# A two-layer linear-attention and expert-selection network on one Trainium2 core: x of tiles 0 and 1 loaded ahead of the weights, their products taken together by weight blocks, state products of two tiles side by side, and the emission order of all stages written anew

## The chip, the cores and the metric

The kernel runs on one NeuronCore of a Trainium2 chip. The metric is the device time of one launch in microseconds (us). Before the change it is 745.13 us, the median of three runs (744.25 to 745.64). TensorE (PE) multiplies, VectorE (DVE), ScalarE (ACT) and GpSimd (POOL) do the elementwise work, SyncE (SP) issues the DMAs. PEld is PE's weight load, which overlaps its matmuls.

## The reference

Four sublayers act on x of 2048 rows and 576 columns: A, B, A, B, with the same weights in both rounds.

```python
def _A_ref(x, wqkv, wo):            # 32 heads of 18
    q, k, v = split_heads(x @ wqkv)
    pq, pk = phi(q), phi(k)         # phi(t) = where(t > 0, t + 1, exp(t)) + 1e-6
    kv = einsum("bhsd,bhse->bhde", pk, v)
    z = einsum("bhsd->bhd", pk)
    num = einsum("bhqd,bhde->bhqe", pq, kv)
    den = einsum("bhqd,bhd->bhq", pq, z)[..., None] + 1e-6
    return merge_heads(num / den) @ wo

def _B_ref(x, w_q, k1, k2, u, v):   # 32 heads, 8 x 8 experts, the best one of each
    s1 = (x @ w_q)[..., :dk] @ k1.T ; s2 = (x @ w_q)[..., dk:] @ k2.T
    e = argmax(s1) * 8 + argmax(s2)
    act = gelu(einsum("nd,nhkd->nhk", x, u[e]))
    return einsum("nhk,nhkd->nd", act, v[e])

x = x + _A_ref(_layernorm(x), A_wqkv, A_wo)
x = x + _B_ref(_layernorm(x), B_w_q, B_k1, B_k2, B_u, B_v)
x = x + _A_ref(_layernorm(x), A_wqkv, A_wo)
x = x + _B_ref(_layernorm(x), B_w_q, B_k1, B_k2, B_u, B_v)
```

The state kv is a sum over all 2048 rows, so the second half of a sublayer A can begin only when the first half is done with every tile.

## The kernel before

The 2048 rows are 16 tiles of 128 rows. Every operand of a product is split into a high part and a low part (`split`, lines 108 to 111: ACT writes the high part, DVE or POOL subtracts it for the low one), and a product is high by high, low by high and high by low: 14 passes of two matmuls each (`product`, lines 213 to 222). The 576 contracted columns are five blocks; block 2 holds 64 columns, its high part in the upper half of the partitions and its low part in the lower half, so that it needs one pass fewer. A weight block reaches its place by a DMA into a staging tile `wst` and a split into `whi` and `wlo`.

For a tile t of layer l the first half ("front") has these pieces. `front_T` (`fT`) transposes the normalised tile on PE (tile `ptf`, line 205) and splits the result into `thif` and `tlof`. `front_k`, `front_v` and `front_q` (`k`, `v`, `q`) form the products `ppk`, `ppv` and `ppq` (line 220); after k and q comes `phi` (lines 226 to 228: Exp on ACT, two DVE instructions) with the results `ek` and `eq`, and v is copied by ACT into one of the two buffers `v5` by the parity of t (lines 251 and 253). `front_state` (`st`, line 291) adds the tile's state product into PSUM tile `kva`: 20 small matmuls whose stationary operand is 128 x 64, where the other products have 128 x 128.

The second half ("back") has `state_mask` (`mk`), `state_sum` (`zs`, tile `z`), `state_fold` (`M`, tile `m`: the state times wo), `back_scale` (`num`: POOL and DVE, result `o`), `back_oT` (`oT`: transposes `pto`) and `back_out` (`O`: product `ppo`, residual, layernorm). Sublayer B has `exp_T` (`bc`: transposes `ptb` of the normalised tile t and of the gate `cg` of tile c), `exp_scores` (`S`: tile `pps`, or the upper half of `kva`, line 444), `exp_gelu` (`gel`), `exp_select` (`sel`: fourteen DVE instructions, the last writes `cg`, line 509) and `exp_out` (`po`). Where a piece yields, its later parts (evictions, splits) are emitted at a later mention of it.

The expert projection is multiplied with k1 and k2 by the kernel itself (`fold_load`, `fold_mm`, `fold_out`, `fold_T`): 64 loads of 288 KB from `in_wq_t`, eight in each of the front's tiles 2 to 9, and small matmuls (line 560) with a stationary operand of 128 x 32.

The order on the engines is the order of emission: `in_order` (lines 150 to 161) chains the instructions of PE, ACT, DVE and POOL one after the other. SP issues its DMAs in the order that the program gives them, each when its staging tile is free, so that a DMA that waits holds those behind it. The order is written by hand in three forms: the start (lines 697 to 734), a loop over the front's tiles 2 to 12 (lines 736 to 761) and texts that `play` (line 676) reads, a word per piece. `step2` (lines 682 to 690), run for s from 5 to 12, does the back of layer 0 for tiles s to s+2 and the front of layer 1 for tile s-3.

PSUM holds four tiles of 1024 columns (`ps`), `kva` one of them while a front runs.

## Time and profile before

| what | us |
|---|---|
| median of the three runs | 745.13 |
| the profiled execution: its own time | 744.04 |
| its span, first to last instruction | 742.2 |
| PE busy in it | 723.5 |
| DVE, ACT, POOL busy | 458.6, 289.7, 200.3 |
| granted TensorE clock, mean | 0.999 |

Read it so: PE is busy for 97% of the span, and the remaining 18.7 us are spread over the start, the changes from one stage to the next, and the end. The stages, by time: the start with tiles 0 and 1 to about 36 us, the front of layer 0 to about 222, the turn to the back with the first tiles to about 306, the eight steps to about 446, the turn to layer 1's back to about 540, and that back to the end. The rows of the profile follow where they are used. A "timeline" row gives the start, the duration, engine, line, what is written from what, the shapes, how many instructions are merged, and in brackets the engine's idle time before and what ended it.

### The profile page before, as it was taken

How to read it: one execution, taken by the hardware profiler on the slowest of the kernel's cores; microseconds unless marked ns; L12 is line 12 of the kernel's file. 1: busy time of each engine (PE TensorE's matmuls, PEld its weight loads, DVE VectorE, ACT ScalarE, POOL GpSimd, SP SyncE). 2: the span in 40 equal slices, each digit the busy share in tenths (PEclk: the TensorE clock that was granted, in tenths of full speed). 3: DMA queues.
4: the chain of work that ended last, by engine and by line, in shares of the span. 5: the costliest groups of instructions: out<-in, count | busy, mean ns of one | idle time of the engine just before them, and what ended most of it. 6: DMA issues, size and time to landing. Idle time of an engine off the chain costs nothing.

```text
span 742.2 us, 14654 instructions
## 1 busy us (share of the span) xinstructions
PE 723.5 (97%) x5672; PEld 673.6 (91%) x5672; DVE 458.6 (62%) x1006; ACT 289.7 (39%) x588; POOL 200.3 (27%) x541
## 2 busy tenths in 40 slices
PE   7999999999999999999999999999999999999995
PEld 5999989999998898999999999999899999999884
DVE  4532342324337886666666665662466899999986
ACT  5422333223234545444444444352333433444343
POOL 2210000001003543333333333230033334433431
PEclk9999999999999999999999999999999999999999
DMA  9736456631121322223332222212624323121101
GB/s 267 259 114 240 160 181 235 212 114 49 49 64 35 110 100 79 90 85 89 107 107 85 84 85 92 71 61 69 180 85 120 105 84 116 37 90 34 49 33 65
DMA packets 52470, 79.64 MB, mean 107 GB/s; under 512 B 5616, under 2 KB 22512, under 8 KB 52400
## 3 DMA queue, kind: packets, MB, share of 16 engines
q1 hardware_dynamic: 52400, 78.70, 33.3%
q8 instruction: 45, 0.74, 0.4%
q14 instruction: 25, 0.20, 0.1%
HBM read 55.12 MB, written 23.56 MB: 106 GB/s over the span
## 4 chain that ended last, share of the span: by engine, by line
PE 82%; DVE 10%; ACT 3%; issue 2%; POOL 1%; DMA 1%; SPq 0%; DVEq 0%; POOLq 0%; ACTq 0%
PE ppk L220 15%; PE ppv L220 15%; PE ppq L220 13%; PE ppo L414 13%; PE pps L444 6%; PE kva L444 5%; PE kva L291 3%; PE fold_ps L560 2%; PE ptb L205 2%; PE ptf L205 2%; PE pto L205 2%; PE po L528 2%; PE m L345 1%; DVE o L392 1%; DVE tlob L111 1%
## 5 line engine op out<-in xcount | busy, mean ns | idle before, releaser
L227 DVE TENSOR_SCALAR ek<-ek 128x576 f32<-128x576 f32 x32 | 14.7, 459 | 82.4 <-ACT ek L226 82.4
L220 PE MATMUL ppk<-whi,thif 128*128 128x252 f32 x320 | 49.6, 299 | 2.1 <-ACT thif L110 2.0
L414 PE MATMUL ppo<-ohi,thio 126*128 126x252 f32 (+1 forms) x320 | 50.3, 299 | 0.1
L220 PEld LDWEIGHTS ppk<-whi,thif 128*128 128x128 f32 x320 | 44.0, 188 | 6.5 <-issue 3.3
L171 POOL TENSOR_SCALAR rsf<-mvf 128x1 f32<-128x1 f32 x16 | 3.0, 190 | 169.7 <-DVE mvf L169 169.5
L227 DVE TENSOR_SCALAR eq<-eq 128x576 f32<-128x576 f32 x32 | 15.6, 488 | 52.6 <-ACT eq L226 52.6
L220 PE MATMUL ppk<-whi,tlof 128*128 128x252 f32 x320 | 47.6, 293 | 0.3 <-DVE tlof L111 0.3
L220 PE MATMUL ppv<-whi,thif 128*128 128x252 f32 x320 | 47.4, 295 | 0.1
L220 PE MATMUL ppv<-whi,tlof 128*128 128x252 f32 x320 | 46.9, 293 | 0.0
L195 ACT ACTIVATE yb<-x,rsb 128x640 f32<-128x640 f32 x32 | 29.5, 923 | 44.1 <-POOL rsb L188 44.1
L414 PEld LDWEIGHTS ppo<-ohi,thio 126*128 126x128 f32 (+1 forms) x320 | 44.8, 189 | 1.1 <-DVE eq L228 0.3
L220 PEld LDWEIGHTS ppk<-whi,tlof 128*128 128x128 f32 x320 | 44.2, 188 | 0.5 <-DVE tlof L111 0.5
L220 PEld LDWEIGHTS ppv<-whi,thif 128*128 128x128 f32 x320 | 43.9, 188 | 0.4 <-ACT thif L110 0.3
L181 ACT ACTIVATE junk<-x,mb 128x576 bf16<-128x576 f32 x32 | 24.7, 770 | 49.5 <-POOL mb L180 46.2
L220 PEld LDWEIGHTS ppv<-whi,tlof 128*128 128x128 f32 x320 | 43.9, 188 | 0.0
L251 ACT ACTIVATE v<-ppv 128x252 f32<-128x252 f32 x64 | 20.9, 379 | 50.1 <-PE ppv L220 48.2
L220 PE MATMUL ppq<-whi 128*128 128x252 f32 (+1 forms) x260 | 39.6, 299 | 0.6 <-DVE eq L228 0.6
L414 PE MATMUL ppo<-olo,thio 126*128 126x252 f32 (+1 forms) x256 | 39.5, 293 | 0.0
L414 PE MATMUL ppo<-ohi,tloo 126*128 126x252 f32 (+1 forms) x256 | 39.4, 293 | 0.0
L220 PE MATMUL ppk<-wlo,thif 128*128 128x252 f32 (+1 forms) x256 | 39.1, 293 | 0.0
L226 ACT ACTIVATE eq<-ppq 128x576 f32<-128x576 f32 x32 | 20.7, 647 | 46.8 <-PE ppq L220 46.8
L404 DVE SCALAR_TENSOR_TENSOR x<-po,x 128x576 f32<-128x576 f32 x29 | 21.9, 754 | 27.4 <-PE po L528 26.4
(162 smaller groups left out, 1794.8 us busy)
## 6 DMA issues: line engine op xcount, KB each, us to landing
fold<-in_wq_t SPq DMA_DIRECT2D x64, 288.0 KB, 4.8
whi<-hl_d SPq DMA_DIRECT2D x26, 320.0 KB, 3.4
pq_d<-eq SPq DMA_DIRECT2D x19, 288.0 KB, 2.1
pq<-pq_d SPq DMA_DIRECT2D x19, 288.0 KB, 3.0
xf<-in_x SPq DMA_DIRECT2D x16, 288.0 KB, 5.4
x<-in_x SPq DMA_DIRECT2D x16, 288.0 KB, 2.9
x_d<-x SPq DMA_DIRECT2D x16, 288.0 KB, 2.4
x<-x_d SPq DMA_DIRECT2D x16, 288.0 KB, 2.8
```

What stands on the lines that cost most here:

```text
L181: nc.scalar.activation(junk, xt, AF.Square, bias=m[:, 0:1], accum_out=m[:, 1:2])
L195: nc.scalar.activation(y, x2, AF.Identity, scale=rs[:, 0:1], bias=rs[:, 1:2])
L205: nc.tensor.transpose(pt[:, b * P:(b + 1) * P], x, ident)
L220: nc.tensor.matmul(o[:, at:at + c1 - c0], tt[a == "lo"][:, b, :], wb[:, cols + c0:cols + c1], start=(i == 0), stop=(i == len(todo) - 1))
L226: nc.scalar.activation(e, row(p), AF.Exp)
L227: nc.vector.tensor_scalar(e, e, 1.0, EPS, op0=ALU.min, op1=ALU.add)
L251: nc.scalar.activation(vt[:, c:c + 4, :63], x.rearrange("p (c e) -> p c e", c=4), AF.Copy)
L291: nc.tensor.matmul(a[64 * h:64 * h + 64, c * 72:c * 72 + n], vt[:, 2 * c + h], fk[:, f0:f0 + n], start=(t == 0 and c == 0), stop=(t == NT ...
L404: nc.vector.scalar_tensor_tensor(y, row(p), 0.0, xt, op0=ALU.add, op1=ALU.add, accum_out=total)
L414: nc.tensor.matmul(p[:, at:at + c1 - c0], hl[a][:r, b], w[:r, c0:c1], start=(i == 0), stop=(i == len(todo) - 1))
L444: nc.tensor.matmul(p[:, :512], hl[a == "lo"][:, b, :], shi[:, b] if w == "hi" else slo[:, blocks(REM)[b][1]], start=(i == 0), stop=(i == l ...
L528: nc.tensor.matmul(p[:, at:at + c1 - c0], c[i], vmix[:, c0:c1], start=(i == 0 and not based), stop=(i == 1))
```

## The change

What it does:

- The start issues the load of x for tile 1 before the first weight block, not after the fifth. `statistics` computes the factor and the offset on POOL for tiles 0 and 1 too, and the normalisation of tile 1 is on DVE instead of ACT. Both tiles are transposed before the products begin.
- k, v and q of tiles 0 and 1 are formed by `pair_product`: the passes are sorted by weight block, and each pass is done for tile 0 and then for tile 1 before the next.
- `st` of tile 1 and, in the loop over the tiles 2 to 9, of each odd tile stands right behind `st` of the even one before it. In the steps it does so too: two old steps make one text of double length, with both `st` in its second half.
- The loop ends with tile 9; tiles 10 to 12 are in the text behind it. All texts are new; most words keep their neighbours. On DVE, in the back of layer 1, `o` of tile 10, `phi` of tiles 11 and 12 and several subtractions and residuals stand some places earlier or later; PE's sequence there differs in the places of a few products and transposes.

```diff
+    def pair_product(t0, t1, cols, n, parts=PARTS):
+
+        o = [psum(f"pp{n}0_{t}") for t in (0, 1)]
+        todo = sorted(passes(REM), key=lambda p: p[1])
+        for i, (a, b, w) in enumerate(todo):
+            wb = whi[:, b] if w == "hi" else wlo[:, blocks(REM)[b][1]]
+            for p, tt in zip(o, (t0, t1)):
+                for c0, c1, at in parts:
+                    nc.tensor.matmul(p[:, at:at + c1 - c0], tt[a == "lo"][:, b, :], wb[:, cols + c0:cols + c1],
+                                     start=(i == 0), stop=(i == len(todo) - 1))
+        return o
...
     def front_k(l, t):
-        k = product(tt["f", l, t], whi, wlo, D, f"k{l}_{t}", by_block=(l == 0 and t == 0))
+        k = pairs.pop(("k", l, t), None)
+        if k is None:
+            k = product(tt["f", l, t], whi, wlo, D, f"k{l}_{t}")
         yield
         tt["fk", l, t] = phi(k, f"k{l}_{t}")
 
+    def front_pair(f, cols, parts=PARTS):
+        pairs[f, 0, 0], pairs[f, 0, 1] = pair_product(tt["f", 0, 0], tt["f", 0, 1], cols, f, parts)
...
-        nc.scalar.activation(y, x2, AF.Identity, scale=rs[:, 0:1], bias=rs[:, 1:2])
+        if vector:
+            nc.vector.tensor_scalar(y, x2, rs[:, 0:1], rs[:, 1:2], op0=ALU.mult, op1=ALU.add)
+        else:
+            nc.scalar.activation(y, x2, AF.Identity, scale=rs[:, 0:1], bias=rs[:, 1:2])
...
+    def pair(t):
+        return ((st, t - 1), (st, t)) if t % 2 else ()
...
     nc.sync.dma_start(ident, c_ident)
+    first_load(0, 1)
     wk_in = load_weight(wqkv, D, REM, "w")
-    first_load(0, 1)
     wv_in = load_weight(wqkv, 2 * D, REM, "w")
...
+        ys["f", 0, 0] = normalized(x0, rs0, "f0_0")
+        ys["f", 0, 1] = normalized(x1, rs1, "f0_1", vector=True)
         split_weight(wk_in, D, whi, wlo, REM, (0,))
...
+        run(0, (fT, 0), (fT, 1, 1))
+        split_weight(wk_in, D, whi, wlo, REM, (1,))
+        run(0, (fT, 1))
+        warm_up(2)
+        split_weight(wk_in, D, whi, wlo, REM, (2,))
         split_weight(wk_in, D, whi, wlo, REM, (3,), nc.gpsimd)
...
+        front_pair("k", D)
         split_weight(wv_in, 2 * D, whi, wlo, REM, (0, 1))
...
+        split_weight(wv_in, 2 * D, whi, wlo, REM, (4,))
+        front_pair("v", 2 * D, PARTS_V)
+        ys["f", 0, 2] = normalized(x2, next(st2), "f0_2")
...
+        front_pair("q", 0)
+        run(0, *pair(1), (q, 0), (q, 1))
+        PER, FIRST = 8, 10
...
-                run(0, (q, t), (fT, t + 1), (st, t))
...
+            run(0, (v, t), (q, t), (fT, t + 1), *pair(t))
...
-        for s in range(5, 13):
-            step2(s)
+        for s in range(5, 13, 2):
+            play("""
+            num0.2 k1.-3x2 v1.-3 num0.2x2 v1.-3 bc0.0,-1 v1.-3 fT1.-2 bc0.0,-1 fT1.-2 keep1.-2 oT0.1x2 S0.0x2 gel0.0
+            po0.-1x3 sel0.0 gel0.0 ld0.3 sel0.0 po0.-1 O0.1x4 sel0.0x2 num0.3 k1.-2x2 v1.-2 oT0.2 num0.3x2 v1.-2
+            bc0.1,0x2 v1.-2 st1.-3 st1.-2 fT1.-1x2 keep1.-1 oT0.2 S0.1x2 gel0.1 po0.0x2 ld0.4 po0.0 sel0.1 gel0.1
+            sel0.1 po0.0 O0.2x4 sel0.1x2
+        """, s)
```

The first place is the head of SP's queue. The names are the tiles written: `xf` is x of a tile, `wst` a staging tile of a weight block (two DMAs for block 2). Before:

```order
L599 DMA xf_152<-in_x 128x576
L699 DMA ident<-in_c_ident 128x128
L134 DMA wst_0_156<-in_wqkv 128x576
L134 DMA wst_1_158<-in_wqkv 128x576
L136 DMA wst_2_160<-in_wqkv 64x576
L137 DMA wst_2_160<-in_wqkv 64x576
L134 DMA wst_3_163<-in_wqkv 128x576
L134 DMA wst_4_165<-in_wqkv 128x576
L599 DMA xf_167<-in_x 128x576
```

And with the change:

```order
L625 DMA xf_152<-in_x 128x576
L717 DMA ident<-in_c_ident 128x128
L625 DMA xf_156<-in_x 128x576
L135 DMA wst_0_158<-in_wqkv 128x576
L135 DMA wst_1_160<-in_wqkv 128x576
L137 DMA wst_2_162<-in_wqkv 64x576
L138 DMA wst_2_162<-in_wqkv 64x576
```

The second x takes the third place, and every k weight block moves one place back.

The second place is PE in the steps, between the v product and the scores of a step. `ptb`, `ptf` and `pto` are transposes, `kva` from `ek` and `v5` is the state product, `kva` from `shi` and `thib` the scores. Before, with the step s = 7:

```order
L205 MATMUL ptb0_7_4294<-ident_66,yb0_7_4203 128x128 x5
L205 MATMUL ptb0_7_4294<-ident_66,cg0_6_4215 128x128
L205 MATMUL ptf1_5_4306<-ident_66,yf0_5_4162 128x128 x5
L291 MATMUL kva1_3582<-ek1_4_4252,v5_0_86 64x72 x8
L291 MATMUL kva1_3582<-ek1_4_4252,v5_0_86 64x36 x2
L205 MATMUL pto0_8_4328<-ident_66,o0_8_3990 128x128 x5
L444 MATMUL kva1_3582<-shi_80,thib0_7_4301 128x512 x5
```

With the change, s = 7, the first half of a double step:

```order
L209 MATMUL ptb0_7_4297<-ident_66,yb0_7_4210 128x128 x5
L209 MATMUL ptb0_7_4297<-ident_66,cg0_6_4222 128x128
L209 MATMUL ptf1_5_4307<-ident_66,yf0_5_4169 128x128 x5
L209 MATMUL pto0_8_4321<-ident_66,o0_8_3983 128x128 x5
L470 MATMUL kva1_3593<-shi_80,thib0_7_4304 128x512 x5
```

And s = 8, its second half:

```order
L209 MATMUL pto0_9_4509<-ident_66,o0_9_4224 128x128 x5
L209 MATMUL ptb0_8_4526<-ident_66,yb0_8_4431 128x128 x5
L209 MATMUL ptb0_8_4526<-ident_66,cg0_7_4443 128x128
L317 MATMUL kva1_3593<-ek1_4_4255,v5_0_86 64x72 x8
L317 MATMUL kva1_3593<-ek1_4_4255,v5_0_86 64x36 x2
L317 MATMUL kva1_3593<-ek1_5_4476,v5_1_87 64x72 x8
L317 MATMUL kva1_3593<-ek1_5_4476,v5_1_87 64x36 x2
L209 MATMUL ptf1_6_4558<-ident_66,yf0_6_4390 128x128 x5
L470 MATMUL kva1_3593<-shi_80,thib0_8_4533 128x512 x5
```

The state product of tile 4 has moved from the first half to the second, where it stands ahead of that of tile 5.

The third place is PE at the turn of layer 1, where the state is complete and is folded with wo (`m`) and summed (`z`). Before:

```order
L291 MATMUL kva1_3582<-ek1_15_6511,v5_1_87 64x72 x8
L291 MATMUL kva1_3582<-ek1_15_6511,v5_1_87 64x36 x2
L345 MATMUL m1_1_6577<-wob1_6468,kvb_83 126x288 x2
L327 MATMUL z1_6580<-zc_69,pick_68 128x4x72
L328 MATMUL z1_6580<-zc_69,pick_68 128x36
L327 MATMUL z1_6580<-zc_69,pick_68 128x4x54
L328 MATMUL z1_6580<-zc_69,pick_68 128x36
L345 MATMUL m1_4_6594<-wob4_6477,kvb_83 128x288 x2
```

With the change:

```order
L317 MATMUL kva1_3593<-ek1_14_6430,v5_0_86 64x72 x8
L317 MATMUL kva1_3593<-ek1_14_6430,v5_0_86 64x36 x2
L317 MATMUL kva1_3593<-ek1_15_6514,v5_1_87 64x72 x8
L317 MATMUL kva1_3593<-ek1_15_6514,v5_1_87 64x36 x2
L353 MATMUL z1_6584<-zc_69,pick_68 128x4x72
L354 MATMUL z1_6584<-zc_69,pick_68 128x36
L353 MATMUL z1_6584<-zc_69,pick_68 128x4x54
L354 MATMUL z1_6584<-zc_69,pick_68 128x36
L371 MATMUL m1_1_6592<-wob1_6389,kvb_83 126x288 x2
```

The four `z` matmuls now stand ahead of the first `m`, and the state product of tile 14 stands directly ahead of that of tile 15; before, the q product of tile 0 was between them.

More of the change, by code (lines that the diff above doesn't have):

```diff
@@ L211, in transposed, with product @@
         return hi, lo
-    def product(tt, hi, lo, cols, n, parts=PARTS, rem=REM, by_block=False):
+    def product(tt, hi, lo, cols, n, parts=PARTS, rem=REM):
         o = psum(f"pp{n}")
-        todo = sorted(passes(rem), key=lambda p: p[1]) if by_block else passes(rem)
+        todo = passes(rem)
         for i, (a, b, w) in enumerate(todo):
@@ L255, in front_q @@
     def front_q(l, t):
-        q = product(tt["f", l, t], whi, wlo, 0, f"q{l}_{t}")
+        q = pairs.pop(("q", l, t), None)
+        if q is None:
+            q = product(tt["f", l, t], whi, wlo, 0, f"q{l}_{t}")
         yield
@@ L734, in network @@
-        run(0, (st, 0), (fT, 2), (v, 1), (q, 0), (st, 1), (q, 1))
-        PER, FIRST = 8, 13
+        first_load(0, 3)
+        for t in v5:
+            nc.gpsimd.memset(t, 1.0)
+        split_weight(wv_in, 2 * D, whi, wlo, REM, (2,))
+        run(0, (k, 0))
+        split_weight(wv_in, 2 * D, whi, wlo, REM, (3,))
+        run(0, (k, 1))
+        x2 = xs.pop(("f", 2))
+        st2 = statistics(x2, "f0_2")
+        next(st2)
+        split_weight(wv_in, 2 * D, whi, wlo, REM, (4,))
+        front_pair("v", 2 * D, PARTS_V)
```

187 lines of the change are left out of this document (84 added, 103 removed).

## The prediction

> **What bounds the kernel now.** I read the page's head first, then a table of windows cut at the stages, then the chain of waits and the timelines of single places. In the table a row gives a stretch, its length, and each engine's busy time with its instructions.
>
> ```profile
> span 742.2 us, 14654 instructions
> PE 723.5 (97%) x5672; PEld 673.6 (91%) x5672; DVE 458.6 (62%) x1006; ACT 289.7 (39%) x588; POOL 200.3 (27%) x541
> ```
>
> ```profile
> core 0: us, PE busy (x) PEld busy (x) DVE busy (x) ACT busy (x) POOL busy (x), PEclk, DMA share, GB/s
> 0.00:36.00 36.00, 32.27 (x235) 26.70 (x236) 19.55 (x35) 17.97 (x31) 8.34 (x22) 1.00 0.87 271
> 36.00:160.00 124.00, 124.00 (x1191) 114.11 (x1190) 40.68 (x86) 36.88 (x86) 9.03 (x27) 1.00 0.55 184
> 160.00:300.00 140.00, 136.34 (x1062) 128.23 (x1062) 82.47 (x172) 55.05 (x113) 36.63 (x92) 1.00 0.22 69
> 300.00:446.00 146.00, 146.00 (x1165) 138.78 (x1165) 96.52 (x220) 65.92 (x134) 50.74 (x142) 1.00 0.28 92
> 446.00:540.00 94.00, 92.33 (x743) 87.69 (x742) 48.85 (x107) 37.89 (x78) 19.93 (x55) 1.00 0.33 97
> 540.00:690.00 150.00, 148.98 (x1029) 140.64 (x1028) 127.22 (x279) 55.76 (x108) 58.80 (x154) 1.00 0.27 83
> 690.00:742.00 52.00, 43.60 (x258) 37.44 (x256) 43.29 (x113) 20.27 (x40) 16.80 (x51) 0.99 0.13 46
> ```
>
> PE bounds every stage but the last. Its idle time is 3.7 us in the start, none in the fold loop and in the steps, 3.7 and 1.7 in the two turns, 1.0 and 8.4 behind 540. Since the change keeps the matmuls, it can gain in two ways: fewer such gaps, and less time lost when PE changes between kinds of matmul (which counts as busy). Behind 540 DVE is busy for 127 of 150 us and hands its lateness to the end; but from 446 to 540 it is busy for 49 of 94, so it is not behind when that stage begins, and what PE gains ahead of 540 moves DVE's work forward too.
>
> **The start.** Rows of PE, ACT, DVE and POOL, each from its timeline:
>
> ```profile
> 9.81 0.53 PE L220 MATMUL ppk<-whi,thif 128*128 128x252 f32 x2 [1.22 <-ACT thif L110]
> ...
> 14.35 0.71 PE L205 MATMUL ptf<-ident,yf 128*128 128x128 f32 x5
> 15.85 1.58 PE L220 MATMUL ppk<-whi,thif 128*128 128x252 f32 x10 [0.79 <-ACT thif L110]
> ```
>
> And from the chain of waits, the k product of tile 2 with its start and length:
>
> ```profile
> 36.74 3.64 PE ppk L220 x28
> ```
>
> ```profile
> 5.84 0.68 ACT L110 ACTIVATE whi<-wst 128x576 fp32r<-128x576 f32 x1 [3.83 <-DMA wst<-in_wqkv]
> ...
> 8.48 0.68 ACT L115 ACTIVATE whi<-wst 128x576 fp32r<-128x576 f32 x1 [0.52 <-DMA wst<-in_wqkv]
> ```
>
> ```profile
> 3.68 0.46 DVE L166 BATCH_NORM_STATS2 stf<-xf 128x6 f32<-128x288 f32 x1 [2.52 <-DMA xf<-in_x]
> ...
> 4.53 0.21 DVE L169 BATCH_NORM_AGGREGATE mvf<-stf 128x2 f32<-128x12 f32 x1
> ...
> 17.90 0.45 DVE L227 TENSOR_SCALAR ek<-ek 128x576 f32<-128x576 f32 x1
> ...
> 24.82 0.21 DVE L169 BATCH_NORM_AGGREGATE mvf<-stf 128x2 f32<-128x12 f32 x1
> ```
>
> ```profile
> 26.06 0.27 POOL L174 TENSOR_SCALAR rsf<-mvf,rsf 128x1 f32<-128x1 f32 x1
> ```
>
> Today tile 0's product starts at 9.81, halts with its weight blocks, and tile 1's transposes stand behind it with a second wait, 0.79. A product takes 3.64, a pass 3.64/14 = 0.26.
>
> With the change x of tile 1 is the third DMA, past the six of the k weight; today's third, a weight block, lets ACT start at 5.84. From then on: statistics 1.06 (3.68 to 4.53 + 0.21), POOL's three instructions 1.30 (25.03 to 26.33), the normalisation on DVE 0.5 (0.45 x 640/576, an estimate; twice that if it ran at half the rate), transposes and ACT's split 1.50 (14.35 to 15.85). Tile 1 can be multiplied at 5.84 + 1.06 + 1.30 + 0.5 + 1.5 = 10.2, say 10.3 with the waits between. The weight blocks come a place later. Blocks 0 and 2 land 2.64 apart today, 1.3 a block, so blocks 0, 1 and 2 now land near 7.2, 8.5 and 9.8, and the later ones at the same pace; a pair uses a block for six passes, 1.56, so none is late. Tile 1's low part waits in DVE's queue behind two weight splits: about 0.3. Then: pair k to 10.0 + 0.3 + 7.28 = 17.6, v to 24.9, transposes of tile 2 to 25.4, q to 32.7, the double state product 1.5 to 1.7: tile 2 starts at 34.4 to 34.7 on the scale on which it starts at 36.74. ACT's split of the first q block stands behind the normalisation of tile 2, which waits for statistics that DVE does behind `phi` of tile 1; by the same durations it ends at 25.0 to 25.3, just in time. I take **-2.0** and keep as ends -2.7 (neither the 0.3 nor a wait at q) and +0.6 (x of tile 1 lands no sooner than today's block 2, 8.48: 2.6 later).
>
> **State products side by side.** Rows of PE, of ACT and of the table of waits:
>
> ```profile
> 488.64 1.43 PE L291 MATMUL kva<-ek,v 128*64 128x72 f32 x40
> ```
>
> ```profile
> 349.94 0.86 PE L291 MATMUL kva<-ek,v 128*64 128x72 f32 x20
> 350.72 0.76 PE L205 MATMUL pto<-ident,o 128*128 128x128 f32 x5
> 351.24 1.40 PE L444 MATMUL kva<-shi,thib 128*128 128x512 f32 x5
> ```
>
> ```profile
> 349.50 0.81 ACT L110 ACTIVATE thib<-ptb 128x768 fp32r<-128x768 f32 x1
> 350.20 0.23 ACT L253 ACTIVATE v<-ppv 128x72 f32<-128x72 f32 x1
> 350.31 0.71 ACT L110 ACTIVATE thif<-ptf 128x640 fp32r<-128x640 f32 x1
> ```
>
> ```profile
> PEld kva L291 <- issue: 5.0, 30, 0.2
> ```
>
> The first row is a pair that the kernel already has, the next ones a single visit in a step, the last one PEld's waits. Twenty matmuls more cost 1.43 - 0.86 = 0.57, yet a visit occupies PE from 349.94 to 350.72, 0.78: some 0.12 to 0.2 is lost on leaving, and 5.0/30 = 0.17 on entering. A visit saved is worth 0.12 where the fold matmuls behind it (a third kind) pay the entry instead, else 0.29. Of 30 visits 19 remain: four go in the loop (**-0.5**), two in tiles 10 to 13 (**-0.6**), one at the turn of layer 1 (**-0.3**), four in the steps. In a first half without it the scores could start at 349.94 - 0.17 + 0.52 (from `pto` to the scores) = 350.29; ACT's split `thib` ends at 350.31 today, and the third copy of v (0.11 between the starts at 350.20 and 350.31) now stands ahead of it: 350.42 and a little, a wait of 0.17, with `thif` and `thio` queued behind it on ACT, which PE wants later. So a double step gains 0.12, the four **-0.5** (between 0 and -1.2).
>
> The Trainium skill, page TensorEngine Tiling (Array Packing), section Key Properties, says that a change of tiling mode, and not merely of the tile, drains the engine; its page TensorE: Matmul & The Clock Gate, section Single matmul latency, puts a drain near 175 ns. By these an estimate gives a visit 0.35 with both changes and 0.175 in the loop, and a sum 0.6 larger; the rows above show the entry at that price and the exit at less.
>
> **The turns.** Rows of PE's timeline, in the order in which they are used:
>
> ```profile
> 176.06 1.18 PE L220 MATMUL ppq<-whi,thif 128*128 128x252 f32 x7 [0.51 <-DVE ek L228]
> ```
>
> ```profile
> 259.95 0.30 PE L205 MATMUL ptb<-ident,cg 128*128 128x128 f32 x1 [0.87 <-DVE cg L509]
> ```
>
> ```profile
> 297.38 0.97 PE L444 MATMUL kva<-shi,thib 128*128 128x512 f32 x3 [0.70 <-ACT thib L110]
> ```
>
> ```profile
> 527.34 0.81 PE L291 MATMUL kva<-ek,v 128*64 128x72 f32 x20
> 529.70 1.21 PE L345 MATMUL m<-wob,kvb 127*126 127x288 f32 x4 [1.54 <-issue]
> ```
>
> ```profile
> 223.31 0.72 PE L327 MATMUL z<-zc,pick 128*128 128x288 f32 x2 [0.63 <-ACT zc L310]
> ...
> 224.60 3.16 PE L345 MATMUL m<-wob,kvb 127*126 127x288 f32 x12
> ```
>
> Tiles 10 to 12: the fold transposes move ahead of q, so that `ek` of tile 11 no longer shares ACT and DVE with their splits; the 0.51 should go: **-0.5** (0 to -0.65). At 259.95 PE waits for `cg`; now the 3.7 us product `ppo` of tile 3 stands ahead of it, and at 297.38 the transposes of tile 2 (0.5, today later) fill part of the 0.70. Together 1.4; but `po` of tile 0 then comes about 1.1 after the transposed `cg`, whose two splits wait behind others: **-1.0** (0 to -1.5). At 529.70 PE waits 1.54 for DVE's masked state with `z` still to do; in layer 0, where `z` goes first, it waits 0.63, does `z` in 1.29, and `m` follows without a wait: **-0.9** (0 to -1.2).
>
> **The sum.** -2.0 - 0.5 - 0.6 - 0.3 - 0.5 - 0.5 - 1.0 - 0.9 = -6.3. The new texts also reorder DVE, ACT and SP at some forty places, most with no effect; for one short new wait, of the size of those above, I give back 0.5: **-5.8**. The last stage I cost at nothing: DVE covers what PE gains there, and the same DVE work follows. If a moved DVE instruction waits, that cover is gone and the wait reaches the end whole. The profiled execution took 744.04, 1.1 below the median of 745.13; it becomes 738.2, and on the scale of the median **739.3**.
>
> **Rivals.** *The turns and the steps give nothing* (a filled wait returns at the next instruction: `thib` in the steps, `cg`'s split on DVE): the start, the loop and tiles 10 to 13 remain, -3.1, 742.0. For it: ACT's queue at 350.31 has no slack. Against: `z` ahead of `m` is shown by layer 0. Chance 0.15. *The start does not do what it says*, since x of tile 1 is as late as 8.48: -5.8 + 2.6, 742.0 to 742.5. For it: DMA is at 0.87 of its engines there. Against: the third load lands at 5.84. Chance 0.10. *All low ends together*: -2.7 - 0.5 - 0.6 - 0.3 - 1.2 - 0.65 - 1.5 - 1.2 = -8.6, 736.5. For it: no row forbids one of them. Against: eight at once. Chance 0.08. *Slower*: DVE's strict order in the last stage. There `o` of tile 10, `phi` of tiles 11 and 12 and several subtractions change places, and one that comes too early holds the whole queue; the longest DVE wait there now is this:
>
> ```profile
> DVE x L404 <- PE ppo L414: 4.7, 3, 3.3
> ```
>
> It decides from 7.3 us on (the 5.8 gained and the 1.5 of a measurable loss): three waits of 3.3, 745.13 - 5.8 + 9.9 = 749.2. For it: DVE has 23 us of slack in 150, so lateness isn't made up. Against: PE's order there is nearly the old one. Chance 0.09. A gain that stays within measurement, 0.04.
>
> **The numbers.** The forecast has 0.54. A change of 0.2%, 1.5 us, is what a measurement tells from none. Faster: 0.54 + 0.13 + 0.10 + 0.08 = 0.85; within: 0.02 of the first rival, 0.01 of the last, and 0.04: 0.07; slower 0.08. The range runs from a little below the best case, 736.2, to 743.6, the last measurable gain; the forecast's own is 737.5 to 741.
>
> **What would show it.** Right: a first pair at 10.0 to 10.4 and tile 2's k at 34 to 35; 40-matmul state products; the loop and steps still without a gap, a double step 0.1 to 0.3 shorter than two steps; `m` of layer 1 without a wait. Wrong: an x of tile 1 that DVE takes up behind 7, `whi` of q waited for at 25, new PE waits for `thib` above 0.3 in each step, or DVE waits above 3 us behind 600.

## The result, and the profile after

The changed kernel takes 733.65 us (median of 4 runs, 733.06 to 733.75), the kernel before 745.06 beside it (4 runs, 744.25 to 745.64). The ratio is 0.9845, 95% interval 0.9833 to 0.9857: 11.4 us less, about twice the 5.8 forecast, and below the range. The profiled execution took 733.06, its span is 731.3.

The head of the page after:

```profile
span 731.3 us, 14661 instructions
PE 717.8 (98%) x5674; PEld 672.5 (92%) x5674; DVE 453.6 (62%) x1005; ACT 288.5 (39%) x587; POOL 201.0 (27%) x543
```

PE's busy time fell by 5.7 (723.5 to 717.8), its idle time by 5.2 (18.7 to 13.5). The table of windows after, cut at the same places of the program (a stretch, its length, each engine's busy time and instructions, clock, DMA):

```profile
core 0: us, PE busy (x) PEld busy (x) DVE busy (x) ACT busy (x) POOL busy (x), PEclk, DMA share, GB/s
0.00:34.30 34.30, 31.58 (x225) 26.61 (x227) 19.81 (x33) 17.63 (x31) 9.33 (x24) 1.00 0.92 276
34.30:157.80 123.50, 123.50 (x1207) 113.74 (x1204) 41.34 (x88) 36.47 (x86) 9.11 (x27) 1.00 0.56 187
157.80:293.40 135.60, 134.41 (x1066) 128.26 (x1065) 78.48 (x170) 55.08 (x113) 34.59 (x90) 1.00 0.23 71
293.40:438.60 145.20, 145.20 (x1166) 138.48 (x1165) 97.50 (x222) 64.97 (x134) 51.82 (x146) 1.00 0.28 93
438.60:531.80 93.20, 91.80 (x741) 87.23 (x739) 48.98 (x107) 38.28 (x78) 19.90 (x54) 1.00 0.33 98
531.80:680.00 148.20, 148.20 (x1031) 140.87 (x1030) 124.84 (x279) 55.82 (x108) 60.03 (x155) 1.00 0.28 84
680.00:731.00 51.00, 43.07 (x256) 37.28 (x255) 42.67 (x111) 20.22 (x40) 16.20 (x50) 0.98 0.13 47
```

The third stretch (tiles 10 to 15 and the turn of layer 0) has 1.2 of PE's idle time where it had 3.7, and the last stage up to 680 has none where it had 1.0. The chain of waits says the same: its shares by engine before,

```profile
PE 82%; DVE 10%; ACT 3%; issue 2%; POOL 1%; DMA 1%; SPq 0%; DVEq 0%; POOLq 0%; ACTq 0%
```

and after:

```profile
PE 93%; DVE 2%; ACT 2%; DMA 1%; issue 1%; POOL 0%; SPq 0%; DVEq 0%; POOLq 0%; ACTq 0%
```

DVE hardly holds the end any more. Where the time went is read by laying the starts of the same products in the two timelines side by side:

| start of | before | after | difference | gained in the stretch | forecast |
|---|---|---|---|---|---|
| k of tile 2, layer 0 (start) | 36.58 | 34.87 | -1.71 | -1.7 | -2.0 |
| k of tile 10 (loop) | 154.49 | 152.32 | -2.16 | -0.45 | -0.5 |
| q of tile 14 (tiles 10 to 13) | 227.38 | 223.45 | -3.93 | -1.8 | -1.1 |
| k of tile 2, layer 1 (turn of layer 0) | 306.35 | 299.72 | -6.63 | -2.7 | -1.0 |
| k of tile 12, layer 1 (steps) | 480.06 | 472.30 | -7.77 | -1.1 | -0.5 |
| q of tile 4, layer 1 (its turn) | 564.81 | 555.77 | -9.04 | -1.3 | -1.2 |
| the last instruction's end | 739.22 | 728.33 | -10.90 | -1.9 | 0 |

All columns are in us, and a negative number is a gain. Start, loop and turn of layer 1 came out near the forecast; nothing was given back. Tiles 10 to 13, the steps, and above all the turn of layer 0 and the last stage gained more.

### The profile page after: what moved, and what is told of

Read it like the earlier page. It is cut to its first block, busy times and chain, and to the rows that moved or that the text cites. A ratio compares the mean times of both kernels' runs of the same rounds, so it can differ in the third digit from the quotient of the medians.

```text
span 731.3 us, 14661 instructions
## 1 busy us (share of the span) xinstructions
PE 717.8 (98%) x5674; PEld 672.5 (92%) x5674; DVE 453.6 (62%) x1005; ACT 288.5 (39%) x587; POOL 201.0 (27%) x543
## 4 chain that ended last, share of the span: by engine, by line
PE 93%; DVE 2%; ACT 2%; DMA 1%; issue 1%; POOL 0%; SPq 0%; DVEq 0%; POOLq 0%; ACTq 0%
PE ppk L224 15%; PE ppq L224 15%; PE ppv L224 15%; PE ppo L440 15%; PE pps L470 9%; PE kva L470 5%; PE ptb L209 3%; PE kva L317 3%; PE fold_ps L586 2%; PE ptf L209 2%; PE pto L209 2%; PE po L554 2%; PE m L371 1%; PE ppq L236 1%; PE ppk L236 1%; DMA wst<-in_wqkv 1%
## 5 line engine op out<-in xcount | busy, mean ns | idle before, releaser
L224 PE MATMUL ppk<-whi,thif 128*128 128x252 f32 (+1 forms) x300 | 45.7, 299 | 0.8 <-ACT thif L111 0.8
L224 PEld LDWEIGHTS ppk<-whi,thif 128*128 128x128 f32 x300 | 40.9, 188 | 4.5 <-issue 3.3
L224 PE MATMUL ppv<-whi,thif 128*128 128x252 f32 (+1 forms) x300 | 44.3, 294 | 0.1
L224 PE MATMUL ppv<-whi,tlof 128*128 128x252 f32 (+1 forms) x300 | 43.9, 293 | 0.0
L224 PE MATMUL ppk<-whi,tlof 128*128 128x252 f32 (+1 forms) x300 | 43.9, 293 | 0.0
L224 PEld LDWEIGHTS ppv<-whi,thif 128*128 128x128 f32 x300 | 41.2, 188 | 0.4 <-ACT thif L111 0.3
L224 PEld LDWEIGHTS ppk<-whi,tlof 128*128 128x128 f32 x300 | 41.2, 188 | 0.0
L410 POOL TENSOR_TENSOR o<-pq,zb 128x576 f32<-128x576 f32 x19 | 27.4, 1445 | 42.1 <-ACT zb L356 19.4
L111 ACT ACTIVATE thib<-ptb 128x768 fp32r<-128x768 f32 (+2 forms) x37 | 26.9, 727 | 28.6 <-PE ptb L209 28.3
L112 DVE TENSOR_TENSOR tlob<-ptb,thib 128x768 fp32r<-128x768 f32 (+2 forms) x37 | 31.2, 844 | 11.0 <-ACT thib L111 10.7
```

The lines of the kernel that those rows point to most:

```text
L111: nc.scalar.activation(hi, src, AF.Copy)
L112: eng.tensor_tensor(lo, src, hi.bitcast(F32), op=ALU.subtract)
L224: nc.tensor.matmul(o[:, at:at + c1 - c0], tt[a == "lo"][:, b, :], wb[:, cols + c0:cols + c1], start=(i == 0), stop=(i == len(todo) - 1))
L410: nc.gpsimd.tensor_tensor(o[:, :D], pq, zb, op=ALU.mult)
```

## The experiments

Between two executions the timelines behind the start agree to some hundredths of a us at most places (to 0.2 at one, near 640), so a single move is read from the starts of PE's products, relative to the product ahead of it. The old start itself varies: k of tile 2 begins between 36.40 and 38.17 in the profiled executions of the kernels with the unchanged old start, between 34.84 and 35.25 with the new one. The latest, 38.17, is that of g2, where PE was granted 0.72 of its clock from 10 to 16; the other old starts had 1.00. The medians of single moves carry this.

### The four parts, put back one at a time

Each kernel is the changed one with one old part. The main places of the edits (in e1 the old statistics, normalisation and order of the splits go back with them; "..." stands for the rest of a text):

```diff
# e1_old_start
-    first_load(0, 1)
     wk_in = load_weight(wqkv, D, REM, "w")
+    first_load(0, 1)
-        front_pair("k", D)
+        run(0, (k, 0, 1), (fT, 1))
# e2_old_first: the old loop, and the old text up to the steps
-        PER, FIRST = 8, 10
+        PER, FIRST = 8, 13
# e3_old_steps
-        for s in range(5, 13, 2):
+        for s in range(5, 13):
+            step2(s)
# e4_old_last: the old text behind the steps
-            M1.1x2 M1.4 ...
+            mk1.0 M1.1 zs1.0 ...
```

> The changed kernel with the old start put back (x of tile 1 behind the k weight, single products of tiles 0 and 1). Theory A (the differences read from the two traces are losses of PE that reach the end unchanged): 1.7 lost, 735.4. Theory B (the terms as they were predicted): 2.0 lost, 735.7. Theory C (a later wait swallows what the start gains): less than 1.0 lost, below 734.7.

> The changed kernel with the old fold loop and the old text of tiles 13 to 15 and of layer 0's turn. Theory A (traces): 0.5 in the loop, 1.7 in tiles 10 to 13, 2.7 in the turn, 4.9 lost: 738.6. Theory B (predicted terms): 0.5 + 0.6 + 0.5 + 1.0 = 2.6 lost: 736.3. Theory C (waits only shift, a later stage swallows them): below 735.5.

> The changed kernel with the eight single steps in place of four double ones. Theory A (a visit saved is worth its whole 0.28, no wait for the split of the transposed expert rows): 4 x 0.28 = 1.1 lost, 734.8. Theory B (predicted: a wait of 0.17 takes more than half of it back): 0.5 lost, 734.2. Theory C: nothing lost, 733.7.

> The changed kernel with the old last text (turn of layer 1 and the last stage). Theory A (traces): 1.3 in the turn and 1.9 behind it, 3.2 lost: 736.9. Theory B (predicted: the turn gives 1.2, the last stage is set by DVE and gives nothing): 1.2 lost, 734.9. Theory C (the last stage is set by DVE and swallows even the turn): below 734.2.

| kernel | median (range, runs) | over the changed kernel | read from the starts of the products |
|---|---|---|---|
| e1_old_start | 735.07 (734.52 to 736.10, 4) | 1.4 | 2.7 (a late start of 736.10) |
| e2_old_first | 738.02 (737.79 to 738.27, 5) | 4.4 | 4.9 |
| e3_old_steps | 734.42 (733.96 to 734.52, 4) | 0.8 | 1.1 |
| e4_old_last | 736.91 (736.39 to 737.04, 4) | 3.3 | 3.5 |

The medians add up to 9.8, of 10.4 between the changed kernel and the runs of before in this set (744.08, 9 runs). The changed kernel was not run in this set, and the kernel before took 1.0 more beside it (745.06), so a single difference of medians is good to about 1 us. The starts add up to 12.2, of which 1.2 is the old start of e1 being later (37.75) than in the kernel before (36.58): 11.0 are left, of 10.9 between the two timelines. Theory A holds: in these four kernels, what PE gains in one part stays to the end whatever stands behind it. Theory B is out by 1.7 in e2 and by 2.0 in e4, theory C in all four; the medians of e1 and e3 don't part A from B, the starts of the products in e3 do, for A.

### The turn of layer 0: one term, two causes

The prediction had this turn lose 0.87 for `cg` and 0.70 for `thib`, both by PE's order.

```diff
# g1_turn0, on the kernel before
-bc0.-1,0 q0.15 O0.3 S0.1
+q0.15 O0.3 bc0.-1,0 S0.1
-S0.4 po0.3 oT0.5 S0.4 fT1.2
+fT1.2 S0.4 po0.3 oT0.5 S0.4
```

> The kernel before with two moves on PE in the turn of layer 0: the product ppo of tile 3 ahead of the transpose of cg, and the transposes of tile 2 of layer 1 ahead of the scores of tile 4. Theory A (a filled wait is gone for good): 1.1 at the first place and 0.5 to 0.6 at the second, all of it still there at the end: 1.6 to 1.7 less than before. Theory B (as predicted: about half of it comes back at the product po of tile 0 and behind it): 0.8 less.

743.65 beside 744.28 (10 and 21 runs; ratio 0.9989, 0.9974 to 1.0003). By the starts: 1.09 gained at `ppo` of tile 3, and all of it, 1.10, lost at `ppo` of tile 4. PE's timeline of g1 has the new wait, at the scores of tile 2:

```profile
265.43 1.40 PE L444 MATMUL pps<-shi,thib 128*128 128x512 f32 x5 [0.82 <-DVE x L404]
```

The second move gained 0.55 at `ppo` of tile 5, still there up to 640. So at the first place the prediction's fear was too small for PE's move alone; yet the changed kernel has that move and keeps the gain. DVE's timelines show `cg` before,

```profile
258.44 1.37 DVE L509 TENSOR_TENSOR cg<-g,c 128x128 f32<-128x128 f32 x1
```

and after:

```profile
256.02 0.29 DVE L535 TENSOR_TENSOR cg<-g,c 128x128 f32<-128x128 f32 x1
```

The same instruction takes 1.08 more before, and POOL's timeline before has this beside it:

```profile
258.25 1.41 POOL L384 TENSOR_TENSOR o<-pq,zb 128x576 f32<-128x576 f32 x1
```

It ends at 259.66, `cg` at 259.81. DVE counted as busy while POOL held it up. The Trainium skill, page SBUF — State Buffer, section Who interferes with whom, says that a VectorE instruction with two SBUF inputs contends with a GpSimd instruction that reads SBUF, and that the later one blocks until the first is done; these rows agree. To test the hold, POOL's instruction alone was moved:

```diff
# h1_num5, on the kernel before
-sel0.1 num0.5 bc0.-1,0 ... po0.0x2 gel0.1
+sel0.1 bc0.-1,0 ... po0.0x2 gel0.1 num0.5
```

> The kernel before with one move on POOL alone: its 1.41 us multiplication for o of tile 5 stands behind the second part of the gelu of tile 1 instead of ahead of the transpose of cg of tile 0. Theory P (VectorE's instruction for cg takes 1.37 there and 0.29 elsewhere because POOL's multiplication holds it until it ends): cg takes 0.3, PE's wait of 0.87 at 259.95 goes, about 1.0 less than before, still there at the end. Theory B (the order of PE makes that wait, as the prediction had it): cg stays late, nothing gained.

743.66 beside 744.98 (9 and 20 runs; ratio 0.9982, 0.9973 to 0.9992). DVE's timeline of h1:

```profile
258.47 0.29 DVE L509 TENSOR_TENSOR cg<-g,c 128x128 f32<-128x128 f32 x1
...
260.95 1.83 DVE L479 TENSOR_TENSOR m<-s,mx 128x512 bf16<-128x512 f32 x1
```

`cg` takes 0.29, and PE gains 1.06 without any move of its own: theory P at this place. But POOL's instruction, now at 260.79, holds `m` for 1.14 (0.69 elsewhere), and 0.52 comes back at the same scores; about 0.5 is kept, not the 1.0 that theory P had. Next both moves together, and then with DVE's:

```diff
# k2_num5_o3: h1_num5 and PE's first move of g1_turn0
# m1_turn0: k2_num5_o3, and on DVE
-sel0.1 bc0.-1,0 ld0.6 sel0.1 bc0.2,-1
+sel0.1x2 bc0.-1,0 ld0.6 bc0.2,-1
```

> The kernel before with POOL's multiplication for o of tile 5 moved as in h1_num5 and, on PE, the product ppo of tile 3 ahead of the transpose of cg as in g1_turn0. Theory P (cg in time and x of tile 3 early: both are needed): 1.1 less at ppo of tile 3 and still 1.0 to 1.1 at ppk of tile 0 of layer 1. Theory D (other moves keep the gain): 0.5 less there, as with POOL's move alone.

745.95 beside 744.34 (10 and 27 runs; ratio 1.0023, 1.0013 to 1.0033): 1.09 gained and 1.84 lost behind it. Theory P, as I had put it, fell. DVE's timeline of k2:

```profile
263.00 0.29 DVE L111 TENSOR_TENSOR tlob<-ptb,thib 128x128 fp32r<-128x128 f32 x1 [1.59 <-ACT thib L110]
```

With `cg` transposed 3.7 later, DVE waits 1.59 for its split, and the selection and x of tile 3 stand behind that.

> The kernel before with the moves of k2_num5_o3 and, on DVE, the second part of the selection of tile 1 ahead of the split of the transposed cg. Theory P (three queues have to move together): x of tile 3 comes about 1 sooner than in k2, the 1.1 gained at ppo of tile 3 is still there at ppk of tile 0 of layer 1. Theory D (something else of the new order keeps it): 0.3 or less there.

744.37 beside 744.30 (10 and 16 runs; ratio 1.0003, 0.9993 to 1.0013). x of tile 3 now comes in time, and the 1.09 is still there (0.98 of it) at `ppo` of tile 4; then 1.4 is lost ahead of k of tile 0. PE's timeline of m1:

```profile
272.72 0.77 PE L205 MATMUL ptf<-ident,yf 128*128 128x128 f32 x5 [0.70 <-ACT yf L195]
```

The wait has moved on to POOL's and ACT's chain for `yf`. In the changed kernel ACT takes the split `thio` ahead of the squares of tile 3 there, which m1 does not. So this 1.1 belongs to no single move: three queues together carry it past one consumer only, and what carries it past the next is left open; ACT's order there points to a fourth move, which no run here isolates.

The second wait was the other way round. ACT's timeline before:

```profile
289.80 0.78 ACT L181 ACTIVATE junk<-x,mf 128x576 bf16<-128x576 f32 x1 [1.42 <-POOL mf L180]
...
290.58 0.63 ACT L251 ACTIVATE v<-ppv 128x252 f32<-128x252 f32 x2
291.10 0.77 ACT L181 ACTIVATE junk<-x,mb 128x576 bf16<-128x576 f32 x1
...
293.39 0.92 ACT L195 ACTIVATE yb<-x,rsb 128x640 f32<-128x640 f32 x1 [0.77 <-POOL rsb L188]
```

`yb` of tile 4, for which PE waits 0.35 at 294.37, has its squares (`junk` from `mb`) behind those of tile 2 and two copies of v.

```diff
# h3_spread, on the kernel before
-v1.1 sel0.3 po0.2 v1.0 O0.4 sel0.3x2
+v1.1 sel0.3 O0.4 po0.2 v1.0 sel0.3x2
```

> The kernel before with one move: the squares of tile 4 (its spread on POOL and ACT) ahead of those of tile 2 and of the copies of v in the turn of layer 0; PE's order stays. Theory A (ACT's order makes the two waits behind it): the wait of 0.35 for yb at 294.37 goes and most of the 0.70 for thib at 297.38, 0.7 to 1.0 less. Theory B (filled waits come back): less than 0.3.

743.29 beside 744.98 (6 and 20 runs; ratio 0.9980, 0.9967 to 0.9993); by the starts 1.52 gained at `ppo` of tile 5, and 1.35 of it still there at the last product. ACT's timeline of h3, and PE's:

```profile
289.95 0.78 ACT L181 ACTIVATE junk<-x,mb 128x576 bf16<-128x576 f32 x1 [1.42 <-POOL mb L180]
...
292.85 0.94 ACT L195 ACTIVATE yb<-x,rsb 128x640 f32<-128x640 f32 x1
```

```profile
293.99 0.71 PE L205 MATMUL ptb<-ident,yb 128*128 128x128 f32 x5
...
296.01 1.43 PE L444 MATMUL kva<-shi,thib 128*128 128x512 f32 x5
```

Both waits, 1.05 together, are gone: theory A, more than its 0.7 to 1.0. The changed kernel has that order too (ACT takes `junk` from `mb` at 283.30, from `mf` at 285.87). One word, which moves a small piece of ACT and POOL, was worth more than the whole turn in the forecast.

### The last stage: a hold by POOL and the order of PE

DVE's and PE's timelines before, where the changed kernel first gains behind 600:

```profile
610.88 1.34 DVE L475 TENSOR_TENSOR mx<-mt 128x64 f32<-128x64 f32 x1
```

```profile
613.88 0.54 PE L528 MATMUL po<-vmix,tlob 128*128 128x252 f32 x2 [0.33 <-DVE tlob L111]
```

The maximum `mx` takes 1.34 here; after it takes 0.22, and `po` does not wait:

```profile
601.59 0.22 DVE L501 TENSOR_TENSOR mx<-mt 128x64 f32<-128x64 f32 x1
```

POOL's timeline before has its multiplication for o of tile 14 over `mx`:

```profile
610.58 1.56 POOL L384 TENSOR_TENSOR o<-pq,zb 128x576 f32<-128x576 f32 x1
```

Three kernels, on the kernel before:

```diff
# g2_last
-po1.2 oT1.6 po1.2 sel1.13 num1.7 O1.5
+O1.5 po1.2 oT1.6 po1.2 sel1.13 num1.7
# h2_num14
-num1.6 num1.14 S1.13 sel1.13 bc1.3,2 O1.4 q1.15 gel1.13
+num1.6 S1.13 sel1.13 bc1.3,2 O1.4 q1.15 gel1.13 num1.14
# k1_num14_o5: h2_num14 and
-po1.2 oT1.6 po1.2 sel1.13 num1.7 O1.5
+po1.2 O1.5 oT1.6 po1.2 sel1.13 num1.7
```

> The kernel before with one move on PE behind 540: the product ppo of tile 5 ahead of po of tile 2 and of the transposes of tile 6. Theory A (PE's own waits for ACT's and DVE's splits set this stage, not DVE's sum of work): 1.0 less than before, still there at the end. Theory B (as predicted: DVE sets the stage): nothing, within 0.2.

> The kernel before with one move on POOL alone: its multiplication for o of tile 14 of layer 1 behind the first part of the gelu of tile 13 instead of ahead of the scores of tile 13. Theory P (the same hold: the maximum mx takes 1.34 there and 0.23 elsewhere, so the split tlob and the product po behind it are late): PE's waits at 613 to 615 go, 0.9 less than before, still there at the end. Theory B (DVE's sum of work sets this stage, as predicted): nothing, within 0.2.

> The kernel before with POOL's multiplication for o of tile 14 behind the first part of the gelu of tile 13 and, on PE, the product ppo of tile 5 between po of tile 2 and the transposes of tile 6. Theory P (the hold by POOL and the buffer that eq gives back late are both needed): 1.4 less at ppo of tile 5, 0.9 to 1.0 less from ppq of tile 8 on and at the end. Theory D (other moves of the new order make the gain): 0.3 or less, as with POOL's move alone.

g2 was meant as the changed kernel's move, but there `ppo` of tile 5 stands behind `po` of tile 2, not ahead of it. It took 748.75 beside 744.28 (6 and 21 runs; ratio 1.0056, 1.0037 to 1.0076). Of these 4.5 the move explains 2.7: by the starts 1.9 is gained at `ppo` of tile 5 and 4.6 lost at `ppo` of tile 6. Another 1.6 lies in the start, which the move does not touch: in the profiled execution, the fastest of the six, PE was granted 0.72 of its clock from 10 to 16 us. DVE takes `po` of tile 2 ahead of `ppo` of tile 4, so a `po` 3.7 later holds x of tile 4, and PE's timeline of g2 shows the end of that chain:

```profile
630.04 0.77 PE L205 MATMUL ptb<-ident,yb 128*128 128x128 f32 x5 [2.88 <-ACT yb L195]
```

h2 took POOL's hold from `mx`: 744.18 beside 744.98 (10 and 20 runs; ratio 0.9990, 0.9980 to 0.9999), by the starts only 0.12, at `ppo` of tile 5. In its timelines of DVE and PE the hold has gone to `eq`, and the buffer that `eq` gives back is awaited by `ppo` of tile 5:

```profile
612.80 1.45 DVE L227 TENSOR_SCALAR eq<-eq 128x576 f32<-128x576 f32 x1
```

```profile
615.09 1.59 PE L414 MATMUL ppo<-ohi,thio 126*128 126x252 f32 x10 [0.56 <-DVE eq L228]
```

k1 has both moves: 744.09 beside 744.34 (10 and 27 runs; ratio 0.9998, 0.9986 to 1.0011; its profiled start was 0.5 late). By the starts it gains 1.40 at `ppo` of tile 5, as the changed kernel does, 0.92 at q of tile 8, as there, then 0.56 from `ppo` of tile 6 on, and 0.65 at the end, too little for the medians to show. So theory P holds up to q of tile 8, and two thirds of it at the end: by the order of the four buffers, `ppo` of tile 5 now takes an earlier one, and the transposes that need the late one stand 3.7 behind. PE's move without POOL's was not tried. Of the 1.9 that the changed kernel gains in this stage, 1.0 comes here. Another 0.7 comes between 690 and 717, where PE's waits of 0.16 and 0.34 at 697.56 and 698.77 are gone; no run isolates it.

### z ahead of m

```diff
# k3_z, on the kernel before
-mk1.0 M1.1 zs1.0 ldx1.0 lq1.0 zs1.0 M1.1
+mk1.0 zs1.0 ldx1.0 lq1.0 zs1.0 M1.1 M1.1
```

> The kernel before with z ahead of the first m of layer 1. Theory A (the predicted 0.9: m no longer waits 1.54, z waits about 0.6): 0.9 less at m and at the end. Theory B (m or what follows it waits as long elsewhere): 0.3 or less.

743.07 beside 744.34 (10 and 27 runs; ratio 0.9988, 0.9978 to 0.9999). PE's timeline of k3:

```profile
529.05 0.75 PE L327 MATMUL z<-zc,pick 128*128 128x288 f32 x2 [0.54 <-ACT zc L310]
...
530.37 3.16 PE L345 MATMUL m<-wob,kvb 127*126 127x288 f32 x12
```

0.98 at q of tile 1 and 0.28 more at q of tile 2, all kept: 1.3, theory A and a little over it.

### The third copy of v in a double step

The prediction took 0.17 off each first half, because the third copy of v now stands ahead of the split `thib`. ACT's and PE's timelines after:

```profile
307.84 0.24 ACT L277 ACTIVATE v<-ppv 128x72 f32<-128x72 f32 x1
307.96 0.82 ACT L111 ACTIVATE thib<-ptb 128x768 fp32r<-128x768 f32 x1
```

```profile
308.31 0.71 PE L209 MATMUL pto<-ident,o 128*128 128x128 f32 x5
308.84 1.43 PE L470 MATMUL kva<-shi,thib 128*128 128x512 f32 x5
```

`thib` ends at 308.78, the scores start at 308.84, 0.53 behind `pto` as in the old steps (0.52): no wait.

```diff
# g4_copy, on the changed kernel
-bc0.0,-1 v1.-3 fT1.-2 bc0.0,-1 fT1.-2
+bc0.0,-1 fT1.-2 bc0.0,-1 v1.-3 fT1.-2
```

> The changed kernel with the third copy of v behind the split thib instead of ahead of it in the first half of each double step. Theory A (the split is in time, as the changed kernel's step rows suggest: 3.38 for scores that take 3.36 in the other half): at most 0.1 less. Theory B (as predicted: 0.17 of wait in each first half): 4 x 0.17 = 0.7 less.

735.51 (735.34 to 735.70, 4 runs), 1.9 above the changed kernel, which was not run beside it; by the starts 0.60 lost in each double step, 2.4 in all. Both theories had the wrong sign. PE's timeline of g4:

```profile
308.84 0.77 PE L209 MATMUL pto<-ident,o 128*128 128x128 f32 x5 [0.48 <-ACT v L277]
```

The copy is the last reader of `ppv`, and `pto` needs that buffer. What looked like the price of the new order is what makes it possible: without the state product in between, `pto` starts 0.55 behind `ptf` (307.76 to 308.31) where it started 1.42 behind it (349.30 to 350.72), and wants the buffer 0.87 sooner.

### x of tile 1 early, without the pairs

```diff
# g3_x1_single, on the kernel before
+    first_load(0, 1)
     wk_in = load_weight(wqkv, D, REM, "w")
-    first_load(0, 1)
```

> The kernel before with x of tile 1 loaded ahead of the k weight, as in the changed kernel, but with single products as before; DVE's and ACT's orders stay. Theory A (the pair makes the gain, since a weight block then feeds 1.56 us of matmuls instead of 0.78): nothing gained, up to 1.0 more, since each weight block lands a place later. Theory B (the early x makes the gain): the wait of 0.79 ahead of tile 1 goes, 0.8 less.

746.61 beside 744.28 (10 and 21 runs; ratio 1.0024, 1.0011 to 1.0036): 2.3 slower, more than either theory. PE's timeline of g3 still has the wait ahead of tile 1, and its table of windows shows what else went wrong:

```profile
19.14 1.07 PE L220 MATMUL ppk<-whi,thif 128*128 128x252 f32 x6 [0.79 <-ACT thif L110]
```

```profile
6.80:11.70 4.90, 1.99 (x7) 1.03 (x7) 2.09 (x3) 3.48 (x6) 0.00 (x0) 0.77 1.05 285
11.70:16.30 4.60, 4.57 (x18) 4.50 (x19) 2.82 (x7) 2.04 (x3) 3.44 (x6) 0.50 1.04 269
```

ACT splits the first weight block ahead of the normalisation of tile 0, and that block now lands a place later; PE idled for 2.42 ahead of the transposes, and then got half its clock for 4.6 us. In the profiled execution tile 2 starts 3.3 later than before; 4.6 us at half the clock are worth about 2.3 of it (an estimate from these rows), which leaves 1.0, the most that theory A allowed. Theory B had no ground: PE reaches the transposes of tile 1 without a wait for their input both before (14.35) and here (17.64), so the 0.79 behind them was never a wait for x. The early x lets the transposes of tile 1 stand ahead of the product of tile 0; pairs without the early x were not tried, so the 1.7 of the start is not divided between the two.

### All the moves together, and a faster version

```diff
# m2_moves, on the kernel before: m1_turn0 + h3_spread + k3_z + k1_num14_o5
```

> The kernel before with the moves of m1_turn0, h3_spread, k3_z and k1_num14_o5 together; start, loop, tiles 10 to 13 and steps as before. Theory A (PE's removed waits add up): 1.1 + 1.5 + 1.3 + 0.6 = 4.5 less than before, about 740. Theory C (the last stage, set by DVE, takes most of what is gained ahead of it back): less than 2.5. Theory D (m1's part fails): 3.4.

742.15 beside 744.30 (6 and 16 runs; ratio 0.9967, 0.9955 to 0.9979). By the starts, from q of tile 15 to `ppo` of tile 6 in layer 1: 0.42 lost at m1's place, 1.54 gained by h3's move, 1.26 by z, 0.55 by k1's: 2.9. Each as alone, and 3.1 at the last product: theory D, with m1's part not nought but a loss. At the last instruction 2.6 is left, since PE had half its clock behind 734.3 in this execution (0.50; 0.84 before) and its last four matmuls took 0.5 more. The median is only 2.15 lower, within theory C's bound, but the six runs spread over 1.9, as the old start does.

The changed kernel has waits of the same kinds left. In its start q waits for the first split of its weight, which stands behind the normalisation of tile 2; at the turn of layer 1 the state product of tile 13 no longer covers the split of tile 15. PE's timeline after:

```profile
508.33 1.58 PE L224 MATMUL ppk<-whi,thif 128*128 128x252 f32 x10 [0.79 <-ACT thif L111]
```

```diff
# b1_three and b2_three, on the changed kernel
-k1.14x2 st1.13 fT1.15x2 k1.15
+k1.14x2 fT1.15 st1.13 fT1.15 k1.15
-po1.8 gel1.9 oT1.11 S1.15 po1.8 O1.10 sel1.9 O1.11
+po1.8 gel1.9 O1.10 po1.8 sel1.9 oT1.11 S1.15 O1.11
+        split_weight(wq_in, 0, whi, wlo, REM, (0,))
         ys["f", 0, 2] = normalized(x2, next(st2), "f0_2")
         small_loads()
-        split_weight(wq_in, 0, whi, wlo, REM, (0,))
# b2_three also
-        run(0, (k, 1))
         x2 = xs.pop(("f", 2))
         st2 = statistics(x2, "f0_2")
         next(st2)
         split_weight(wv_in, 2 * D, whi, wlo, REM, (4,))
+        run(0, (k, 1))
```

> The changed kernel with three more moves: the split of the first q block ahead of the normalisation of tile 2; the transposes of tile 15 of layer 1 ahead of the state product of tile 13; the squares of tile 10 ahead of the split of tile 11's transposed o. Theory A (each wait removed stays removed): 0.45 + 0.8 + 0.5 = 1.75 less than the changed kernel, 731.9. Theory C (the last stage is set by DVE and takes its part back): 1.25 less, 732.4. Theory B (half of each comes back): 0.9 less, 732.8.

> The changed kernel with the two later moves of b1_three, and in the start the statistics of tile 2 and the last split of the v weight ahead of phi of tile 1, the first split of the q weight ahead of the normalisation of tile 2. Theory A (a wait removed stays removed): 0.6 in the start, 0.7 at tile 15 and 0.2 behind 690 less than the changed kernel, 732.1. Theory B (the start's part moves to the next product): 732.7.

b1: 732.48 (732.28 to 733.03, 4 runs; ratio to before 0.9828, 0.9813 to 0.9842). Its start gained nothing: 0.40 gone at q of tile 1 had come up as 0.34 ahead of q, where the transposes of tile 2 waited longer for their normalised tile. The two later moves gave 0.69 and 0.19 (0.5 expected of the second). b2 moves that tile's statistics too: 731.35 (731.18 to 731.86, 5 runs; ratio to before 0.9826, 0.9812 to 0.9840). That is 2.3 below the changed kernel's median, but the two were not run beside each other; against before it is 13.0 less where the changed kernel was 11.4 less, 1.6 more. By the starts it gains 0.70 in the start, 0.69 and 0.19, the same 1.6: theory A. PE's timeline of b2:

```profile
25.27 0.84 PE L236 MATMUL ppq<-whi,thif 128*128 128x252 f32 x4
...
506.90 1.57 PE L224 MATMUL ppk<-whi,thif 128*128 128x252 f32 x10
```

It is faster than the kernel before, and by the two traces (spans of 729.6 and 731.3) than the changed one.

## Why the prediction was wrong

The two timelines differ by 10.9, 5.1 more than the 5.8 of the forecast. Of the 5.1, 1.9 lies in the last stage, 1.7 in the turn of layer 0, 0.7 in tiles 10 to 13 and 0.6 in the steps; 0.5 is the part that was given back in advance, and the start gained 0.3 less.

- **Direction, start, loop: right.** 1.7 of 2.0, and 0.45 of 0.5. DVE's timeline after has x of tile 1 at 5.54 (forecast 5.84), PE's has tile 1 in the first pair at 10.36 (10.0 to 10.4):

```profile
5.54 0.46 DVE L167 BATCH_NORM_STATS2 stf<-xf 128x6 f32<-128x288 f32 x1 [0.74 <-DMA xf<-in_x]
```

```profile
10.36 0.53 PE L236 MATMUL ppk<-whi,thif 128*128 128x252 f32 x2 [0.32 <-ACT thif L111]
...
25.62 1.19 PE L236 MATMUL ppq<-whi,thif 128*128 128x252 f32 x4
```

The last row is where the start lost its 0.3: four matmuls of q in 1.19, where four take 0.68 elsewhere. The warning was that q's first split comes "just in time"; it came 0.5 late.
- **A visit saved: right in price, wrong in the deduction.** The steps gave 1.14/4 = 0.29 for each visit saved, the full price of the rows (0.12 and 0.17); the "wait of 0.17" for `thib` did not come. In the loop it was 0.11. The estimate of 0.35 beside it, from the Trainium skill's price of a drain (TensorE: Matmul & The Clock Gate, section Single matmul latency), is not borne out.
- **Tiles 10 to 13: a term mis-sized**, 1.1 for 1.8. The wait of 0.51 carried 0.24 of its surroundings: the transposes took 1.21 from their start to that of q (174.85 to 176.06), where PE's timeline after has 0.46. Before and after:

```profile
174.85 0.71 PE L205 MATMUL ptf<-ident,yf 128*128 128x128 f32 x5
```

```profile
171.86 0.71 PE L209 MATMUL ptf<-ident,yf 128*128 128x128 f32 x5
172.32 1.55 PE L224 MATMUL ppq<-whi,thif 128*128 128x252 f32 x10
```

Ahead of q of tile 12 the same step took 0.69 before (188.06 to 188.75); after, the transposes stand elsewhere and take 0.52 (177.51 to 178.03). No run divides this 1.8 further.
- **The turn of layer 0 is the first step that failed**: 1.4 of waits credited at 1.0 by PE's moves. The wait for `cg` came from POOL holding DVE for 1.08 and goes without any move on PE (h1), and the wait for `thib` came from the order of ACT and POOL (h3: 1.5 alone). The reason given for the deduction, that a filled wait returns at `po` of tile 0, was true of PE's move alone (g1 gave 1.10 back) and not of the new order, which moves DVE, POOL and ACT with it; which of these moves carries the 1.1 stays open (m1 lost 1.4 behind it). I had these under "some forty places, most with no effect" and took 0.5 off for them; one of them alone, h3's, was worth 1.35 at the end.
- **The last stage is the second**: "DVE covers what PE gains there" read a share of busy time, 127 of 150 us, as a bound. That busy time contains time in which POOL held DVE (1.1 of the 1.34 at 610.88), and PE's waits were for single splits. The stage gave 1.9, e4 puts 3.3 on it and the turn together, and in m2 the gains made ahead of it (2.5 at q of tile 2) were still there at the last product. The term that was put at nothing consists of 1.0 near 610, of which k1 makes 0.65, and 0.7 behind 690, whose cause is open.
- **The turn of layer 1 came out right by chance**, 1.3 for 1.2: z was worth 1.3 for 0.9, and the 0.3 of the saved visit was eaten by the new wait of 0.79 at k of tile 15.
- **The rivals.** The turns and steps did not give nothing, and DVE's strict order made no new wait above 3 us behind 600. g2 shows that a wait of nearly that size can arise there, on PE: one product one place too early cost 2.7 by the starts, with a wait of 2.88. Even "all low ends together", 736.5, was too high, since no term stood for the last stage or for moves on ACT and POOL.

## What to carry to other kernels

In an order written out by hand, a wait of the bound engine is priced only after its last link has been followed back on each engine in turn: here it stood on POOL once and in the order of ACT and POOL once, where the prediction read PE. Moving one engine's instruction past a wait can merely shift the wait (g1, k2 and g2 wholly, h1 by half) or keep the gain (h3, k3); which of the two it is shows only where the queues behind it are followed to the next consumer, down to who returns the buffer. An instruction much longer than its kind is a wait that the busy share hides: compare it with the same instruction elsewhere before calling its engine the bound.
